# First weights' rounding moved behind two head pairs, the third tile's units on an even grid, and the first pair's differences on VectorE

## The chip, the core and the metric

The kernel runs on one core of one Trainium2 chip. The metric is the device time of one execution in microseconds, lower is better. Before the change it is 1020.40 us in the median of 3 runs (1019.82 to 1021.38).

## The reference

Sliding-window attention over 8 sequences of 576 tokens with 8 heads of 64, followed by a gated feed-forward layer over all 4608 tokens (512 wide, hidden width 1536), all in float32:

```python
scores = scale * np.matmul(q, k.transpose(0, 1, 3, 2))
mask = (rel >= 0) & (rel < window)          # window = 64
scores = np.where(mask, scores, -1000000000.0)
...
out = np.matmul(attn, v)
...
gate = 1.0 / (1.0 + np.exp(-(x @ w_gate)))
val = x @ w_val
return (gate * val @ w_out).astype(np.float32)
```

## The kernel before, in words

The 4608 tokens are cut into 12 tiles of 384. Tiles 0 and 1 are done by plain products; tiles 2 to 11 are done in five pairs, each pair by a Strassen scheme of seven products. Every float32 operand of a large product is split into a rounded part and a remainder, and three matmuls replace one.

**Attention.** A tile has four head pairs; one head pair of one tile is a unit. A unit has three stages. `stage_a` is the scores (`s`, line 201) and the softmax: VectorE masks and finds the minimum (line 219), ScalarE takes the exponentials (line 228), VectorE makes the reciprocals of the sums (lines 234 and 235), and GpSimd multiplies by them (line 237). `stage_b` transposes the result on TensorE (`pp`, line 245), and ScalarE copies it out of PSUM (`pT`, line 250). `stage_c` is the product with V (`oo`, line 262). For tiles 0 and 1 its result is split at once into `x`; for later tiles ScalarE copies it to `xf` (line 269). The PSUM banks of `s`, `pp` and `oo` of tiles 2 and later turn around in one pool of two.

**Weights.** They arrive as 64-bit words and are converted by `conv_a` (ScalarE, lines 111 and 112), `conv_b` (VectorE, lines 120 to 124) and `conv_c` (ScalarE rounds at line 143, VectorE takes the remainder at line 144). The float32 copies are written out again (`w32d`), and for the Strassen scheme `w_sums` reads them back (`a`), makes sums on GpSimd (lines 406 to 409), splits them (lines 143 and 144) and writes them to `wd`, from which `w_load` reads the stationary operands `wt`. All of these DMAs are issued from SyncE's one list.

**Plain tiles.** For tiles 0 and 1 a plan of entries runs over the hidden blocks j: `up` of tile 0 (two halves of 12 matmuls, gate and value, line 297), `down` of tile 0 for the block before (9 matmuls, line 361), `up` of tile 1. The eight units of tiles 2 and 3 are laid between these entries; the numbers say before which entry a stage stands, and .5 means between the two halves. The first unit's transposes stand at 7, which is before the whole `up` of tile 1 for j = 2, its scores at 4.5, its `oo` at 8.

**First Strassen pair.** Tiles 2 and 3 need differences of their `xf` (`x_parts`, lines 424 to 426, and line 434), each of which is then split (`x_split`: line 273 on ScalarE, line 274 on VectorE). The differences `t`, the read-back weights `a`, the converted weights `w32` and the outputs `yo` share one tag of three buffers. The products themselves are line 452, and VectorE adds their parts at line 458.

Each event has a time in the planner (`put`), and the events are written in the order of these times; within an engine a scheduler then settles the list, and `keep_in_program_order` and `issue_after` fix some of it. The change touches `x_parts` and `x_part`, the table of the units' places ahead of `attend`, the time of `conv_c` for the first two weight blocks, and the instruction behind which it must stand.

Of the kernel before, what the change touches and what calls it, by code (L numbers as in the profile page):

```python
# [26 lines left out]
def attn_ffn(ctx: ExitStack, tc: tile.TileContext, qT, kT, vN, w_gate, w_val, w_out, out):  # L27


    nc = tc.nc  # L30
# [48 lines left out]
    marks = {"pT": {}}  # L79
# [191 lines left out]
    def x_split(src, nm, i, eng):  # L271
        x2 = xp.tile([P, 2, TT], F32R, name=f"x_{nm}", tag=f"x{i}")
        hi = nc.scalar.copy(x2[:, 0, :], src)  # L273
        lo = eng.tensor_sub(out=x2[:, 1, :], in0=src, in1=x2[:, 0, :].bitcast(F32))  # L274
        marks[nm] = (hi.ins, lo.ins)
        return x2
# [139 lines left out]
    def t_tile(nm):  # L416
        return mp.tile([P, TT], F32, name=f"t_{nm}", tag="w32", bufs=W32)

    def x_parts(s, c):

        b11, b21, b12, b22 = (xf[(2 * s + b, 2 * a + c)] for b in range(2) for a in range(2))
        t1, t2, t3 = (t_tile(f"{i}_{s}_{c}") for i in range(3))
        eng = nc.gpsimd
        eng.tensor_sub(out=t1, in0=b12, in1=b11)
        eng.tensor_sub(out=t2, in0=b22, in1=t1)
        eng.tensor_sub(out=t3, in0=b22, in1=b12)
        xs[(s, "T", c)] = {"B11": b11, "B21": b21, "B22": b22, "T1": t1, "T2": t2, "T3": t3}

    def x_part(s, n, c):
        src = xs[(s, "T", c)]  # L430
        nm = PRODUCTS[n][1]
        if nm == "T4":
            src["T4"] = src["T2"]
            nc.gpsimd.tensor_sub(out=src["T2"], in0=src["B21"], in1=src["T2"])
        xs[(s, nm, c)] = x_split(src[nm], f"{nm}_{s}_{c}", 2 * n + c, nc.vector)

    def product(s, k, m, n):
# [67 lines left out]
    def put(tm, o, f, *a):  # L505
        events.append((tm, o, f, a))
# [24 lines left out]
    def unit(s, n):  # L531
        return 2 * s + n // 2 % 2, n // 4 + n % 2 * 2

    plan, fill = [], {}
# [5 lines left out]
        if n < NF:  # L540
            plan.append(("up", 1, n))
    at, now = {}, 0.0
    starts = (4, 8, 13, 17, 22, 26, 31, 36, 41)
    for n, (i, nxt) in enumerate(zip(starts, starts[1:])):
        late = 0 if nxt < i + 5 else 0.5 if i + 3 < len(plan) and plan[i + 3][0] == "up" else 1
        for f, x in ((0, i + 0.5), (1, i + 3 + late), (2, nxt)):
            fill.setdefault(x, []).append((f, *unit(1, n)))

    def attend(i):
# [27 lines left out]
    for i in range(KINDS * NF):  # L577
        j, m = divmod(i, KINDS)
        tm = at[("up", 0, max(j, 1))] + ((-10, -2, 6 * j - 0.5) if j < 2 else (-9, -8, 2) if j == 2 else (-14, -12, 2))[m]
        if i < 2:  # L580
            tm = A0 + 11 + 8 * i
        else:
            put(tm - (30 if j == 0 or j == 1 and m < 2 else 6), 2.5, conv_load, i)
        put(tm, 1, conv_a, i)
        put(tm + 2.4, 2, conv_b, i)
        put(tm + 2.5, 2, conv_c, i)

    def last_tile(t, js, ready):

# [17 lines left out]
    for s in range(1, NS):  # L607
        a, b = 2 * s, 2 * s + 1
        for c in range(2):
            put(now - 21 + 10 * c, 5, x_parts, s, c)  # L610
            for n in range(NPR):
                put(now - 19.5 + 10 * c + 1.2 * n, 5.5, x_part, s, n, c)
# [7 lines left out]
        for k in range(NK):  # L620
# [5 lines left out]
            for m in range(2):  # L626
                for n in range(NPR):
                    put(now, 9, product, s, k, m, n)
                    now += PRT
                    if n in (2, 4, 6) and len(downs) > (RESERVE if m else 0) * (k == 1):  # L630
                        j, x = downs.pop(0)
# [11 lines left out]
    for _, _, f, a in events:  # L643
        if f in (conv_a, conv_b, conv_c):
            with ExitStack() as behind:
                j, m = divmod(a[0], KINDS)
                key = j - AHEAD if m < 2 else j - 1
                early = {3: ("1_2",), 2: ("1_3",), 4: ("1_3",), 5: ("1_3",)}.get(a[0], (key,))
                if j == 2 and m < 2:
                    early += tuple(("w", i) for i in (3, 4))  # L650
                for ins in [i for nm in early for i in marks.get(nm, ())]:
                    behind.enter_context(tc.issue_after(ins))
                if a[0] < 2:
                    behind.enter_context(tc.issue_after(marks["pT"][a[0]]))
                f(*a)
        else:
            f(*a)
# [43 lines left out]
```

## Time and profile before

| | us |
|---|---|
| median of 3 runs | 1020.40 |
| the profiled execution, its device time | 1020.06 |
| span of its instructions | 1018.30 |
| TensorE matmuls busy | 985.9 (97%) |
| TensorE weight loads busy | 883.3 (87%) |
| VectorE busy | 662.8 (65%) |
| ScalarE busy | 525.8 (52%) |
| GpSimd busy | 265.7 (26%) |

The span runs from the first instruction to the last; 1.76 us of the device time lie outside it. A busy share is an average over the whole span, so what an engine does in one stage has to be read from a window of that stage. Names in the rows leave the buffer numbers out: `pT` stands for the copies of both heads of all units. "[1.84 <-DVE w L124]" at the end of a row is idle time just before it, and what ended it.

### The profile page before, as it was taken

The numbers are of one execution on the slowest core, as the hardware profiler recorded it, in microseconds if no ns is written. First come the engines' busy times: TensorE is split into PE (matmuls) and PEld (weight loads), VectorE is DVE, ScalarE is ACT, GpSimd is POOL, SyncE is SP. The second block draws the span as 40 slices with busy tenths as digits, with TensorE's granted clock in tenths as the row PEclk, the third lists the DMA queues.
The fourth block names the chain that finished last, engine by engine and source line by source line (L and its number), as shares of the span: only waits on it lengthen the run. The fifth ranks groups of instructions, "written<-read, shape, count | busy, mean of one in ns | idle before, by whom it ended". The sixth has DMA issues, their size and how long they took to land.

```text
span 1018.3 us, 19859 instructions
## 1 busy us (share of the span) xinstructions
PE 985.9 (97%) x6984; PEld 883.3 (87%) x6984; DVE 662.8 (65%) x1810; ACT 525.8 (52%) x1409; POOL 265.7 (26%) x287
## 2 busy tenths in 40 slices
PE   6889999999999999999999999999999999999998
PEld 4689998878899878989988989988989988999996
DVE  6889897637776764756675776675666577344532
ACT  6878886636564544535454654454555454311122
POOL 4200103567662240212132221213212124010100
PEclk9999999999999999999999999999999999999999
DMA  9899886989998624766642776660766652466500
GB/s 303 283 327 363 309 285 214 355 274 355 372 336 295 207 74 153 249 211 216 205 159 74 234 231 204 223 195 32 237 223 215 212 185 73 143 219 204 190 32 32
DMA packets 126243, 221.51 MB, mean 218 GB/s; under 512 B 9408, under 2 KB 82624, under 8 KB 126144
## 3 DMA queue, kind: packets, MB, share of 16 engines
q1 hardware_dynamic: 126144, 220.24, 65.4%
q8 instruction: 56, 0.92, 0.4%
q14 instruction: 43, 0.35, 0.1%
HBM read 178.52 MB, written 41.68 MB: 216 GB/s over the span
## 4 chain that ended last, share of the span: by engine, by line
PE 75%; DVE 7%; DMA 7%; ACT 5%; issue 2%; POOL 2%; SPq 0%; POOLq 0%; DVEq 0%; ACTq 0%
PE pr L452 40%; PE y L361 23%; PE ph L297 4%; PE oo L262 3%; PE s L201 3%; ACT p L228 2%; PE pp L245 2%; DMA wt<-wd 1%; DMA a<-w32d 1%; DVE w L124 1%; DMA w32d<-w 1%; DVE p L219 1%; DMA out_dram<-yo 1%; DVE w L122 1%; DMA hd<-hh 1%
## 5 line engine op out<-in xcount | busy, mean ns | idle before, releaser
L452 PE MATMUL pr<-x_T,wt 128*128 128x384 f32 x1440 | 288.7, 340 | 5.0 <-DVE c L458 3.3
L452 PEld LDWEIGHTS pr<-x_T,wt 128*128 128x128 f32 x1440 | 251.0, 188 | 21.3 <-DVE c L458 5.2
L361 PE MATMUL y<-w,hh 128*128 128x512 f32 x804 | 250.0, 392 | 0.0
L452 PE MATMUL pr<-x_B,wt 128*128 128x384 f32 x1080 | 221.0, 341 | 0.2
L452 PEld LDWEIGHTS pr<-x_B,wt 128*128 128x128 f32 x1080 | 187.9, 188 | 7.8 <-ACT g L307 1.5
L237 POOL TENSOR_TENSOR p<-p,rs 128x384 f32<-128x384 f32 x92 | 79.5, 865 | 401.5 <-DVE rs L235 374.9
L361 PEld LDWEIGHTS y<-w,hh 128*128 128x128 f32 x804 | 148.6, 188 | 21.3 <-ACT hh L326 1.4
L361 PE MATMUL y<-w,hl 128*128 128x512 f32 x402 | 158.6, 395 | 0.7 <-DVE hl L330 0.7
L458 DVE TENSOR_TENSOR u<-pr,p 128x384 f32<-128x384 f32 x120 | 66.6, 555 | 131.9 <-PE pr L452 128.1
L228 ACT ACTIVATE p<-p,mn 128x128 f32<-128x128 f32 x288 | 110.6, 393 | 78.0 <-DVE mn L219 77.8
L330 POOL TENSOR_TENSOR hl<-h,hh 128x384 fp32r<-128x384 f32 x60 | 64.6, 1076 | 240.1 <-DVE hh L328 231.2
L297 PE MATMUL ph<-x,w 128*128 128x384 f32 x576 | 109.6, 343 | 1.7 <-DVE w L144 1.3
L297 PEld LDWEIGHTS ph<-x,w 128*128 128x128 f32 x576 | 100.8, 191 | 4.9 <-DVE w L144 1.6
L361 PEld LDWEIGHTS y<-w,hl 128*128 128x128 f32 x402 | 75.3, 187 | 19.5 <-DVE hl L330 3.4
L219 DVE CUSTOM_DVE_ANT_0 p<-s,m 128x128 f32<-128x128 f32 x288 | 65.3, 285 | 36.1 <-PE s L201 30.6
L463 ACT COPY p<-pr 128x384 f32<-128x384 f32 x60 | 28.3, 471 | 89.6 <-PE pr L452 82.7
L458 DVE TENSOR_TENSOR c<-pr,u 128x384 f32<-128x384 f32 x120 | 66.6, 555 | 12.1 <-PE pr L452 5.8
L250 ACT COPY pT<-pp 128x384 f32<-128x384 f32 x96 | 42.1, 481 | 48.6 <-PE pp L245 48.5
L330 DVE TENSOR_TENSOR hl<-hb,hh 128x384 fp32r<-128x384 f32 x60 | 39.1, 663 | 40.5 <-ACT hh L326 40.0
L311 DVE SCALAR_TENSOR_TENSOR g<-g,e 128x384 f32<-128x384 f32 x96 | 53.7, 571 | 6.8 <-ACT e L308 4.0
L262 PEld LDWEIGHTS oo<-pT,v 128*64 128x64 f32 x1152 | 39.1, 139 | 20.8 <-ACT pT L250 10.7
L274 DVE TENSOR_TENSOR x_T<-t,x_T 128x384 fp32r<-128x384 f32 x40 | 39.3, 999 | 27.1 <-ACT x_T L273 27.1
(73 smaller groups left out, 1212.2 us busy)
## 6 DMA issues: line engine op xcount, KB each, us to landing
wt<-wd SPq DMA_DIRECT2D x210, 512.0 KB, 4.2
v<-in_vN_dram SPq DMA_DIRECT2D x48, 384.0 KB, 4.4
wd<-ws SPq DMA_DIRECT2D x48, 256.0 KB, 4.8
k<-in_kT_dram SPq DMA_DIRECT2D x48, 224.0 KB, 4.2
q<-in_qT_dram SPq DMA_DIRECT2D x48, 192.0 KB, 3.9
wd<-w SPq DMA_DIRECT2D x36, 256.0 KB, 6.5
out_dram<-yo SPq DMA_DIRECT2D x36, 256.0 KB, 2.1
raw<-in_moe_w_gate_dram SPq DMA_DIRECT2D x12, 512.0 KB, 5.4
```

Source lines behind the costliest of these rows:

```text
L219: nc.vector.tensor_tensor_reduce(out=pt[:, u, :], in0=sc[h][:, u, :], in1=masks[key], op0=ALU.add, op1=ALU.min, scale=-SCALE, scalar=3.0e3 ...
L228: exp = nc.scalar.activation(pt[:, u, :], pt[:, u, :], AF.Exp, bias=mn[:, u:u + 1], scale=-1.0, **sums)
L237: eng.tensor_mul(out=pt, in0=pt, in1=rs.unsqueeze(2).broadcast_to([P, UP, P]))
L250: cp = nc.scalar.copy(pT, pp)
L262: pe(nc.tensor.matmul(oo[h * BLK:(h + 1) * BLK, U * BLK:(U + 1) * BLK], vt[:, U, h * BLK:(h + 1) * BLK], pT[h][:, U // 2, half * BLK:(half ...
L274: lo = eng.tensor_sub(out=x2[:, 1, :], in0=src, in1=x2[:, 0, :].bitcast(F32))
L297: pe(nc.tensor.matmul(ph, l, r, start=i == 0, stop=i == len(prs) - 1))
L311: nc.vector.scalar_tensor_tensor(out=g, in0=g, scalar=1.0, in1=e, op0=ALU.add, op1=ALU.mult)
L330: return eng.tensor_sub(out=h_lo, in0=h32, in1=h_hi.bitcast(F32))
L361: pe(nc.tensor.matmul(yb[y], l, r, start=first and n == 0, stop=last and n == 2))
L452: pe(nc.tensor.matmul(ps, l, r, start=new and i == 0, stop=i == len(prs) - 1, skip_group_check=not new))
L458: nc.vector.tensor_add(out=o, in0=ps, in1=a)
```

## The change

Three edits. `conv_c` of the first two weight blocks gets a later time in the planner and must be issued behind the transposes' copy of the head pair after the one named before. The table of places of the eight units is written out; the scores of three units move from between the halves to behind both (8.5 to 9, 17.5 to 18, 26.5 to 27), and the transposes of five units move by half an entry (7 to 7.5, 11.5 to 12, 20.5 to 21, 29.5 to 30, 34.5 to 35). The four differences of `x` for each of the two column halves go to VectorE for the first Strassen pair; the later pairs keep GpSimd.

```diff
@@ -416,11 +416,14 @@
     def t_tile(nm):
         return mp.tile([P, TT], F32, name=f"t_{nm}", tag="w32", bufs=W32)
 
+    def t_engine(s):
+        return nc.vector if s == 1 else nc.gpsimd
+
     def x_parts(s, c):
 
         b11, b21, b12, b22 = (xf[(2 * s + b, 2 * a + c)] for b in range(2) for a in range(2))
         t1, t2, t3 = (t_tile(f"{i}_{s}_{c}") for i in range(3))
-        eng = nc.gpsimd
+        eng = t_engine(s)
         eng.tensor_sub(out=t1, in0=b12, in1=b11)
         eng.tensor_sub(out=t2, in0=b22, in1=t1)
         eng.tensor_sub(out=t3, in0=b22, in1=b12)
@@ -431,7 +434,7 @@
         nm = PRODUCTS[n][1]
         if nm == "T4":
             src["T4"] = src["T2"]
-            nc.gpsimd.tensor_sub(out=src["T2"], in0=src["B21"], in1=src["T2"])
+            t_engine(s).tensor_sub(out=src["T2"], in0=src["B21"], in1=src["T2"])
         xs[(s, nm, c)] = x_split(src[nm], f"{nm}_{s}_{c}", 2 * n + c, nc.vector)
 
     def product(s, k, m, n):
@@ -540,10 +543,9 @@
         if n < NF:
             plan.append(("up", 1, n))
     at, now = {}, 0.0
-    starts = (4, 8, 13, 17, 22, 26, 31, 36, 41)
-    for n, (i, nxt) in enumerate(zip(starts, starts[1:])):
-        late = 0 if nxt < i + 5 else 0.5 if i + 3 < len(plan) and plan[i + 3][0] == "up" else 1
-        for f, x in ((0, i + 0.5), (1, i + 3 + late), (2, nxt)):
+    for n, at_plan in enumerate(((4.5, 7.5, 8), (9, 12, 13), (13.5, 16, 17), (18, 21, 22),
+                                 (22.5, 25, 26), (27, 30, 31), (31.5, 35, 36), (36.5, 40, 41))):
+        for f, x in enumerate(at_plan):
             fill.setdefault(x, []).append((f, *unit(1, n)))
 
     def attend(i):
@@ -583,7 +585,7 @@
             put(tm - (30 if j == 0 or j == 1 and m < 2 else 6), 2.5, conv_load, i)
         put(tm, 1, conv_a, i)
         put(tm + 2.4, 2, conv_b, i)
-        put(tm + 2.5, 2, conv_c, i)
+        put(tm + (2.5 if i > 1 else 3.5), 2, conv_c, i)
 
     def last_tile(t, js, ready):
 
@@ -651,7 +653,7 @@
                 for ins in [i for nm in early for i in marks.get(nm, ())]:
                     behind.enter_context(tc.issue_after(ins))
                 if a[0] < 2:
-                    behind.enter_context(tc.issue_after(marks["pT"][a[0]]))
+                    behind.enter_context(tc.issue_after(marks["pT"][a[0] + (f is conv_c)]))
                 f(*a)
         else:
             f(*a)
```

ScalarE at the first weights, before (`x` and `pT` of unit 0 and 1, the exponentials `p_0_3` of unit 3, `w_0_422` the first rounded weights):

```order
L273 CAST x_0_415<-oo_0_402 128x384
L250 COPY pT_0_1_434<-pp_0_1_430 128x384
L143 CAST w_0_422<-w_0_0_397 128x512
L250 COPY pT_0_1_440<-pp_0_1_436 128x384
L228 ACTIVATE p_0_3_442,rs_0_3_444<-p_0_3_442,mn_0_3_443 128x128 x3
L228 ACTIVATE p_0_3_454<-p_0_3_454,mn_0_3_455 128x128 x3
L111 ACTIVATE w_1_0_548<-raw_0_233 128x512
```

and now:

```order
L273 CAST x_0_415<-oo_0_402 128x384
L250 COPY pT_0_1_428<-pp_0_1_424 128x384
L250 COPY pT_0_1_434<-pp_0_1_430 128x384
L228 ACTIVATE p_0_3_436,rs_0_3_438<-p_0_3_436,mn_0_3_437 128x128 x3
L228 ACTIVATE p_0_3_448<-p_0_3_448,mn_0_3_449 128x128 x3
L143 CAST w_0_475<-w_0_0_397 128x512
L111 ACTIVATE w_1_0_548<-raw_0_233 128x512
```

The rounding `CAST w_0` stood between the two copies `pT_0_1`; it now stands behind both of them and behind the six exponentials of head pair 3.

TensorE at the transposes of the first unit of tile 2, before (`pp_2_0` the transposes, `ph_1_2` the gate and value halves of `up` for tile 1, j = 2):

```order
L245 MATMUL pp_2_0_1183<-ident,p_2_0_1055 128x128 x3
L245 MATMUL pp_2_0_1189<-ident,p_2_0_1067 128x128 x3
L297 MATMUL ph_1_2_1201<-x_0_708,w_2_988 128x384 x3
L297 MATMUL ph_1_2_1201<-x_1_761,w_2_988 128x384 x3
L297 MATMUL ph_1_2_1201<-x_2_835,w_2_988 128x384 x3
L297 MATMUL ph_1_2_1201<-x_3_864,w_2_988 128x384 x3
L297 MATMUL ph_1_2_1218<-x_0_708,w_2_1011 128x384 x3
L297 MATMUL ph_1_2_1218<-x_1_761,w_2_1011 128x384 x3
L297 MATMUL ph_1_2_1218<-x_2_835,w_2_1011 128x384 x3
L297 MATMUL ph_1_2_1218<-x_3_864,w_2_1011 128x384 x3
```

and now:

```order
L297 MATMUL ph_1_2_1183<-x_0_708,w_2_988 128x384 x3
L297 MATMUL ph_1_2_1183<-x_1_761,w_2_988 128x384 x3
L297 MATMUL ph_1_2_1183<-x_2_835,w_2_988 128x384 x3
L297 MATMUL ph_1_2_1183<-x_3_864,w_2_988 128x384 x3
L245 MATMUL pp_2_0_1200<-ident,p_2_0_1055 128x128 x3
L245 MATMUL pp_2_0_1206<-ident,p_2_0_1067 128x128 x3
L297 MATMUL ph_1_2_1218<-x_0_708,w_2_1011 128x384 x3
L297 MATMUL ph_1_2_1218<-x_1_761,w_2_1011 128x384 x3
L297 MATMUL ph_1_2_1218<-x_2_835,w_2_1011 128x384 x3
L297 MATMUL ph_1_2_1218<-x_3_864,w_2_1011 128x384 x3
```

The six transposes moved from ahead of both halves to between them; the product `oo` that follows the second half has not moved.

GpSimd behind the sums of k = 1 of the gate weights (`sw_1`, `ws_0_1`), before (`t_1_0` and `t_1_1` the differences of `x` for the two column halves):

```order
L144 TENSOR_TENSOR ws_0_1_2758<-sw_1_2748,ws_0_1_2758 128x512
L424 TENSOR_TENSOR t_1_0_2876<-xf_0_1758,xf_0_1255 128x384
L425 TENSOR_TENSOR t_1_0_2877<-xf_2_2024,t_1_0_2876 128x384
L426 TENSOR_TENSOR t_1_0_2878<-xf_2_2024,xf_0_1758 128x384
L434 TENSOR_TENSOR t_1_0_2877<-xf_2_1525,t_1_0_2877 128x384
L406 TENSOR_TENSOR sw_1_2896<-a_1_1_2893 128x256
L408 TENSOR_TENSOR sw_1_2896<-a_1_1_2892,a_1_1_2893 128x256
L407 TENSOR_TENSOR sw_1_2896<-sw_1_2896,a_1_1_2892 128x256
L409 TENSOR_TENSOR sw_1_2896<-a_1_1_2892,sw_1_2896 128x256
L144 TENSOR_TENSOR ws_1_1_2901<-sw_1_2896,ws_1_1_2901 128x512
L424 TENSOR_TENSOR t_1_1_3019<-xf_1_2798,xf_1_2257 128x384
L144 TENSOR_TENSOR ws_1_1_2906<-sw_1_2896,ws_1_1_2906 128x512
```

GpSimd now, from the same instruction on:

```order
L144 TENSOR_TENSOR ws_0_1_2746<-sw_1_2736,ws_0_1_2746 128x512
L406 TENSOR_TENSOR sw_1_2896<-a_1_1_2893 128x256
L408 TENSOR_TENSOR sw_1_2896<-a_1_1_2892,a_1_1_2893 128x256
L407 TENSOR_TENSOR sw_1_2896<-sw_1_2896,a_1_1_2892 128x256
L409 TENSOR_TENSOR sw_1_2896<-a_1_1_2892,sw_1_2896 128x256
L144 TENSOR_TENSOR ws_1_1_2901<-sw_1_2896,ws_1_1_2901 128x512
```

VectorE now, for the first column half (`t_1_0` the differences, `x_T_1_0` their remainders):

```order
L427 TENSOR_TENSOR t_1_0_2876<-xf_0_1758,xf_0_1255 128x384
L428 TENSOR_TENSOR t_1_0_2877<-xf_2_2024,t_1_0_2876 128x384
L274 TENSOR_TENSOR x_T_1_0_2939<-t_1_0_2876,x_T_1_0_2939 128x384
L429 TENSOR_TENSOR t_1_0_2878<-xf_2_2024,xf_0_1758 128x384
L274 TENSOR_TENSOR x_T_1_0_2931<-t_1_0_2877,x_T_1_0_2931 128x384
L437 TENSOR_TENSOR t_1_0_2877<-xf_2_1525,t_1_0_2877 128x384
L274 TENSOR_TENSOR x_T_1_0_2950<-t_1_0_2878,x_T_1_0_2950 128x384
L274 TENSOR_TENSOR x_T_1_0_2980<-t_1_0_2877,x_T_1_0_2980 128x384
```

Eight instructions left GpSimd's list, and VectorE's list has each of them ahead of the remainder that needs it.

In the three units whose scores moved, ScalarE's list also has the six conversions of one weight block (lines 111 and 112) ahead of the exponentials that they stood behind.

## Rows read from the trace of the kernel before

**Rows 1.** Busy us (xcount) of PE, PEld, DVE, ACT, POOL; clock; DMA share; GB/s.

```profile
80.00:160.00 80.00, 80.00 (x612) 73.70 (x611) 71.77 (x198) 68.63 (x155) 10.12 (x10) 1.00 0.89 308
```

**Rows 2.** The same view of two stretches at the lower clock.

```profile
20.00:23.30 3.30, 3.30 (x41) 2.85 (x41) 2.47 (x18) 3.30 (x11) 0.83 (x1) 0.50 1.10 346
...
207.70:211.00 3.30, 3.30 (x17) 2.61 (x12) 0.91 (x1) 0.99 (x2) 1.97 (x3) 0.50 0.90 305
```

**Rows 3.** TensorE's waits, 0 to 80 us: total, times, longest.

```profile
PE pp L245 <- POOL p L237: 5.3, 4, 2.8
...
PE oo L262 <- ACT pT L250: 4.3, 4, 2.5
```

**Rows 4.** TensorE's waits, 160 to 300 us: total, times, longest.

```profile
PE oo L262 <- ACT pT L250: 3.3, 3, 1.7
```

**Rows 5.** Timeline of ScalarE, 16 to 22 us (start, length, work, wait).

```profile
16.30 0.46 ACT L250 COPY pT<-pp 128x384 f32<-128x384 f32 x1
18.60 0.62 ACT L143 CAST w<-w 128x512 fp32r<-128x512 f32 x1 [1.84 <-DVE w L124]
...
21.54 0.67 ACT L111 ACTIVATE w<-raw 128x512 f32<-128x512 f32 x1
```

**Rows 6.** Chain that ended last, 19 to 73 us (start, length, step).

```profile
19.60 2.04 ACT p L228 x9
...
31.70 0.88 PE s L201 x22
...
71.28 1.10 POOL p L237
```

**Rows 7.** Timeline of TensorE, 19 to 78 us.

```profile
19.65 1.33 PE L262 MATMUL oo<-pT,v 128*64 128x64 f32 x22 [2.51 <-ACT pT L250]
...
35.75 2.36 PE L297 MATMUL ph<-x,w 128*128 128x384 f32 x12
...
69.12 0.49 PE L245 MATMUL pp<-ident,p 128*128 128x128 f32 x3
72.42 0.55 PE L245 MATMUL pp<-ident,p 128*128 128x128 f32 x3 [2.81 <-POOL p L237]
72.73 4.42 PE L297 MATMUL ph<-x,w 128*128 128x384 f32 x24
77.08 0.92 PE L262 MATMUL oo<-pT,v 128*64 128x64 f32 x24
```

**Rows 8.** Timeline of TensorE, 175 to 240 us.

```profile
175.12 0.88 PE L201 MATMUL s<-k,q 64*64 64x128 f32 x22 [1.45 <-ACT xf L269]
...
193.78 8.46 PE L361 MATMUL y<-w,hb 128*128 128x512 f32 x36
...
206.71 1.46 PE L262 MATMUL oo<-pT,v 128*64 128x64 f32 x24 [1.74 <-ACT pT L250]
208.10 11.90 PE L361 MATMUL y<-w,hb 128*128 128x512 f32 x45
...
223.91 1.23 PE L452 MATMUL pr<-x_B,wt 128*128 128x384 f32 x6
...
239.45 0.91 PE L262 MATMUL oo<-pT,v 128*64 128x64 f32 x22 [0.46 <-ACT pT L250]
```

**Rows 9.** Timeline of GpSimd, first group of differences.

```profile
200.86 1.01 POOL L424 TENSOR_TENSOR t<-xf,xf 128x384 f32<-128x384 f32 x1 [8.58 <-DMA out_dram<-yo]
...
204.74 0.99 POOL L434 TENSOR_TENSOR t<-xf,t 128x384 f32<-128x384 f32 x1 [0.49 <-DVE x_T L274]
```

**Rows 10.** Timeline of ScalarE behind these differences.

```profile
205.76 0.51 ACT L273 CAST x_T<-t 128x384 fp32r<-128x384 f32 x1 [0.97 <-POOL t L434]
206.18 0.85 ACT L250 COPY pT<-pp 128x384 f32<-128x384 f32 x2
```

**Rows 11.** Tile x_T, 195 to 230 us: ns min/median/max.

```profile
L274 DVE TENSOR_TENSOR x_T<-t,x_T x8: 559/1004/1409, 202.4 to 223.9; 128x384 fp32r<-128x384 f32 x8
```

**Rows 12.** ScalarE's groups by line and form, 100 to 160 us.

```profile
L111 ACT ACTIVATE w<-raw 128x512 f32<-128x512 f32 x14 | 9.1, 665 | 0.0
```

## The prediction

> **What bounds the kernel now.** The table of busy times by stretch comes first, because shares of the whole span mix stages. From 80 to 160 us, in the plain tiles, TensorE is busy 80.00 of 80 us, while VectorE has 71.77, ScalarE 68.63 and the DMA engines 0.89 [rows 1]. There TensorE sets the pace and the others have about a tenth to spare. The long Strassen part behind 300 us is not touched by the change, and I carry it over as it is. What can be won are the waits of TensorE in two places, so the lists of its waits come next. Up to 80 us the largest is transposes that wait for GpSimd's product with the reciprocals, 5.3 us in 4 waits, the longest 2.8; then `oo` that waits for ScalarE's copies `pT`, 4.3 us in 4, the longest 2.5 [rows 3]. From 160 to 300 us it is again `oo` for `pT`, 3.3 us in 3 [rows 4]. The timelines then say what stood ahead of the late instruction on its own engine. Each engine takes its list in order here: a row that waits holds back ready work behind it.
>
> **First weights.** ScalarE copies the first half of `pT` at 16.30 us and then stands 1.84 us for the remainder arithmetic of the weights (VectorE, line 124), rounds them in 0.62 us at 18.60, and only then copies the second half [rows 5]. TensorE's `oo` waits 2.51 us for that copy and goes on at 19.65 [rows 7]. In the new list the copy and six exponentials go first, 2.04 us of work [rows 6], which covers the whole 1.84 us. TensorE's own 2.51 us are not what is won: the chain that ended last runs from 19.60 us over these exponentials on ScalarE, through VectorE, to the scores at 31.70 [rows 6]. So ScalarE's idle time is the price, 1.84 us at most and nothing at least, should another link (the loads, or VectorE's list) be late next. The remainder of the weights, which moves back with the rounding, is first needed by the gate products at 35.75 us [rows 7] and is covered. I take **-1.6**, near the upper end, since the following chain consists of compute steps whose inputs come from the same chain.
>
> **Even grid.** The first unit's transposes do three matmuls at 69.12 us and then stand 2.81 us for GpSimd's product, which runs from 71.28; the transposes go on at 72.42 [rows 6, 7]. Behind them 24 matmuls of `up` take 4.42 us before `oo` at 77.08 [rows 7]. Now 12 of them, half of 4.42, 2.2 us, stand ahead of the transposes, and the wait shrinks to 2.81 - 2.2 = 0.6. What is late next is `pT`, which must be copied within the other 2.2 us instead of 4.4; ScalarE is 86% busy there, so a few tenths may come back. Bounds: 0, if the product slips by as much as TensorE gains, and -2.81. I take **-2.0**. The other moved stages stand in the stretch without any wait [rows 1], so there is nothing to gain at once; their risk is the third rival.
>
> Behind 72 us TensorE is then 3.6 us early. It keeps this only if the conversions follow. They are tied to TensorE's progress through the plan, and the tenth to spare on VectorE and ScalarE makes up 3.6 us within 40; I let it pass whole to 160 us.
>
> **Start of the Strassen part.** Scores wait 1.45 us at 175.12 us for `xf`, which stands on ScalarE behind roundings of GpSimd's sums [rows 8]. Three groups of conversions now come ahead of exponentials, the last one just before this place, so the sums can be read back earlier relative to TensorE. Between 0 and -1.45 I take half, **-0.7**.
>
> The differences: GpSimd starts them at 200.86 us when the outputs have left their buffers, and needs until 204.74 + 0.99 = 205.73 us for four [rows 9]. ScalarE rounds the last one at 205.76 and then copies `pT` at 206.18 [rows 10], for which `oo` had stood 1.74 us until 206.71 [rows 8]. On VectorE the last difference is the sixth instruction (four differences, two remainders). The shortest remainder of this size takes 0.559 us [rows 11], six of them 3.35, so it ends at 204.2 instead of 205.7: -1.5. The whole wait of 1.74 is the other end. But the start at 200.86 hangs on outputs that go through SyncE's list behind the writes of the sums, and if these gain less than TensorE, a part of the wait returns; the lower end is 0. I take **-1.1**. For the second half, GpSimd is rid of four more instructions of 1.0 us [rows 9], which only lets sums and weight loads come earlier; at nothing.
>
> The Trainium skill ("SBUF — State Buffer", section "Who interferes with whom") speaks against this move: a VectorE instruction with two inputs in SBUF and a GpSimd instruction that reads SBUF block each other whole. The remainders beside GpSimd's work, 0.559 alone and up to 1.409 us [rows 11], agree with it; by that rule the four differences of the second half, which run beside GpSimd's sums, would give back up to 4 x 0.85 us, and those of the first half nothing, since GpSimd has nothing else to do then.
>
> **Sum.** -1.6 - 2.0 - 0.7 - 1.1 = -5.4. The profiled execution took 1020.06 us (span 1018.30 and 1.76 around it), 0.34 less than the median of 1020.40. 1020.06 - 5.4 = 1014.7, or 1015.0 from the median; I say **1014.8 us**.
>
> **Rivals.**
>
> *The gain is absorbed before the products.* TensorE comes early, but the sums, their write-out and the weight loads form a chain of their own over GpSimd, DMA and SyncE's list. For it speaks that the loads of product weights now stand behind writes of more sums, and that `oo` waits for `pT` behind such roundings again at 239.45 [rows 8]. Against it: the chain starts from conversions that follow TensorE, and GpSimd lost eight instructions. If only half of the first two terms and none of the last two come through, -1.8: 1018.3. Chance 0.20, range 1016.8 to 1019.3, half of it beyond what can be told from no change.
>
> *The low clock goes with the waits.* TensorE was granted 0.50 (1.2 of 2.4 GHz) from 20 to 23.3 and from 207.7 to 211.0 us [rows 2], each just behind one of the waits above. In the second stretch 45 matmuls took 11.90 us, against 36 in 8.46, which is 10.6 for 45 [rows 8]; with `oo` it cost about 1.5. If the wait at 206.71 goes whole (0.6 more than I took) and the low clock with it: -5.4 - 0.6 - 1.5 = -7.5, 1012.6. The Trainium skill ("TensorE: Matmul & The Clock Gate", section "HAM oscillation — how this bites in real kernels") describes this tie of waits to the half rate. Against it: a wait of about a microsecond likely stays there, and the stretch at 20 us is off the chain. Chance 0.17, range 1010.5 to 1012.8.
>
> *Softmax too late in the moved units (slower).* In three units ScalarE now makes six conversions of 0.665 us [rows 12], 4.0 us, ahead of the exponentials, while scores and transposes move by 2.2 us only. The product with the reciprocals comes up to 4.0 us later against transposes 2.2 later. It decides from the point where softmax had less than 1.8 us in hand; if these units end up like the first one, with 2.81 each [rows 7], that is +8.4 - 5.4 = +3.0, 1023.1. Against it: TensorE has no wait at all between 80 and 160 us, and ScalarE has 11 of these 80 us to spare [rows 1]. Chance 0.08.
>
> *The shared access costs what TensorE gains at the products.* By the row of remainders, four differences at 1.409 instead of 0.559 us delay the second half's parts by 3.4 us, about what GpSimd's faster list gives them; then the last two terms are lost: -3.6, 1016.5. The rule that would do this is the one of the Trainium skill's "SBUF — State Buffer" named above. Chance 0.05.
>
> The forecast itself has 0.50, with 1012.8 to 1016.8 as its own range. About 0.2% of the time, 2.0 us, can be told from no change. Faster than 1018.4: 0.50 + 0.17 + 0.05 + half of 0.20 = 0.82. Same: 0.10. Slower: 0.08. The range from 1010.5 to 1019.3 leaves out the slow case and some edges.
>
> **What would show it.** Right: TensorE's `oo` of the second head pair starts near 17.5 us without its 2.5 us wait, the gate products of tile 0 start about 1.6 us earlier than at 35.75 [rows 7]; the wait at the first unit's transposes is below 1 us; TensorE reaches the first Strassen product near 218.5 instead of 223.91 [rows 8]; on VectorE the first four differences last about 0.56 us. Wrong: new waits of `pp` for line 237 or of `oo` for `pT` between 80 and 160 us, or a wait of products for `wt` or `x_T` behind 215 us. If TensorE is early by 3 us at 160 and not at 240, the first rival is it.

## The result, and the profile after

| | before | changed |
|---|---|---|
| median of 20 runs each, us | 1020.02 | 1022.85 |
| lowest to highest, us | 1018.01 to 1025.25 | 1019.74 to 1026.15 |
| profiled execution, us | 1020.06 | 1021.26 |

The ratio is 1.0023 (95% interval 1.0013 to 1.0033): 0.23% slower. The forecast was 1014.8, and its range ended at 1019.3. The waits that the prediction named did shrink, but others came. First TensorE's waits in the changed kernel, from 0 to 80 us and, behind the dots, from 160 to 300 us; they answer to [rows 3, 4].

```profile
PE s L201 <- DMA k<-in_kT_dram: 6.2, 3, 3.9
PE pp L245 <- POOL p L237: 2.7, 3, 1.0
PE oo L262 <- ACT pT L250: 1.0, 2, 0.7
...
PE s L201 <- ACT xf L269: 2.8, 2, 2.6
PE pp L245 <- POOL p L237: 2.6, 2, 1.8
PE oo L262 <- ACT pT L250: 2.2, 1, 2.2
PE pr L455 <- DVE c L461: 1.8, 3, 1.1
```

Up to 80 us `pp` and `oo` wait 3.7 us together instead of 9.6; the scores' wait for the loads of `k` has grown, from 4.9 us to 6.2. Behind 160 us there is a wait of `pp` for GpSimd that [rows 4] did not have, and the scores' wait for `xf` has grown. TensorE's timeline places them and answers to [rows 7, 8] (the last bracket is the wait in front of the row and what ended it):

```profile
16.83 1.82 PE L262 MATMUL oo<-pT,v 128*64 128x64 f32 x24 [0.72 <-ACT pT L250]
34.85 2.35 PE L297 MATMUL ph<-x,w 128*128 128x384 f32 x12
70.27 0.55 PE L245 MATMUL pp<-ident,p 128*128 128x128 f32 x3 [1.02 <-POOL p L237]
131.46 1.29 PE L262 MATMUL oo<-pT,v 128*64 128x64 f32 x24 [1.27 <-ACT pT L250]
174.69 1.55 PE L201 MATMUL s<-k,q 64*64 64x128 f32 x22 [2.58 <-ACT xf L269]
237.18 0.91 PE L262 MATMUL oo<-pT,v 128*64 128x64 f32 x22 [2.20 <-ACT pT L250]
250.13 0.55 PE L245 MATMUL pp<-ident,p 128*128 128x128 f32 x3 [1.83 <-POOL p L237]
268.46 0.55 PE L245 MATMUL pp<-ident,p 128*128 128x128 f32 x3 [0.76 <-POOL p L237]
```

The wait at the first unit's transposes is 1.02 instead of 2.81 us. But at 131 us, in a stretch that had no wait [rows 1], `oo` now waits 1.27 us; the scores wait 2.58 instead of 1.45; and at 250 and 268 us the transposes stand behind GpSimd.

How early TensorE is follows from the same timelines: the start of the n-th matmul of a kind, less that of the same matmul before. `ph` are the gate and value matmuls, `pr` the products; the heads give the start in the kernel before. The experiments are in the same table. Minus is earlier.

| kernel | ratio (95%) | 145th ph 77.92 | 361st ph 134.15 | 541st ph 180.20 | 1st pr 223.91 | 73rd pr 242.38 | 361st pr 318.49 |
|---|---|---|---|---|---|---|---|
| changed | 1.0023 (1.0013-1.0033) | -4.23 | -1.47 | +0.96 | -2.87 | -2.27 | +1.00 |
| e1 weights | 0.9979 (0.9963-0.9994) | -1.20 | -1.20 | -1.47 | -4.41 | -0.98 | -1.34 |
| e2 grid | 0.9999 (0.9984-1.0014) | -3.69 | -0.93 | +1.03 | -2.83 | -1.81 | -1.87 |
| e3 differences | 1.0038 (1.0020-1.0057) | -0.01 | -0.01 | -0.15 | -3.27 | +1.42 | +4.92 |
| e4 weights, grid | 0.9993 (0.9977-1.0008) | -5.52 | -3.01 | +0.74 | -3.11 | -0.53 | -1.33 |
| e5 changed, order mended | 0.9988 (0.9978-0.9997) | -3.16 | -0.76 | -0.36 | -4.22 | -1.14 | -1.43 |
| e6 before, order swapped | 1.0058 (1.0040-1.0076) | +0.48 | +0.48 | -0.16 | -3.22 | -0.31 | +6.06 |
| e7 changed, first half | 0.9973 (0.9962-0.9984) | -4.65 | -2.25 | +0.29 | -3.57 | -1.68 | -2.56 |
| e8 differences, order mended | 1.0000 (0.9989-1.0012) | +0.39 | +0.39 | -0.27 | -3.72 | +0.51 | +0.15 |
| e9 e7, `xf` first | 1.0028 (1.0016-1.0041) | -5.34 | -2.75 | -4.67 | -6.21 | -6.43 | +3.29 |
| e10 e7, `pT` first | 0.9995 (0.9983-1.0007) | -5.36 | -2.80 | -0.23 | -4.08 | -4.59 | -2.64 |
| e11 e7, both first | 1.0028 (1.0013-1.0043) | -4.63 | -2.21 | -4.14 | -5.06 | -5.25 | +2.91 |
| e12 e7, first unit alone | 0.9944 (0.9928-0.9961) | -4.50 | -3.52 | -3.50 | -6.70 | -5.40 | -5.45 |
| e13 weights, first unit | 0.9979 (0.9965-0.9993) | -4.09 | -3.17 | -3.76 | -6.02 | -3.49 | -3.32 |
| e14 later units alone | 1.0045 (1.0029-1.0060) | +1.65 | +4.51 | +8.22 | +4.45 | +9.17 | +8.29 |
| e15 e12, all differences, order mended | 0.9968 (0.9955-0.9981) | -4.62 | -3.72 | +0.10 | -3.75 | -1.74 | -1.98 |

The leads are those of one profiled execution each; the ratios are of the timed runs against runs of the kernel before on the same chip. How much of a lead belongs to the execution and not to an edit is read from e6, whose lists are those of the kernel before on every engine up to 245 us. It is 1.62 us early at the 73rd `ph` (57.65), 0.48 late at the 145th, and 3.22 early at the first product, because `oo` waits 0.35 us there instead of 1.74 [rows 8] and the 45 matmuls behind it take 10.49 us instead of 11.90 (TensorE's timeline of e6):

```profile
205.06 1.29 PE L262 MATMUL oo<-pT,v 128*64 128x64 f32 x24 [0.35 <-ACT pT L250]
206.29 10.49 PE L361 MATMUL y<-w,hb 128*128 128x512 f32 x45
```

So the column of the first product holds about 3 us that the profiled execution of the kernel before lost by itself; the lists of e3 and e8 are unchanged up to 200 us, and they too are 3.27 and 3.72 early. Elsewhere too a lead under 1.6 us in one trace does not by itself show what an edit did. The executions of e2 and e10 are the fastest of their twelve (1018.07 and 1017.79 us), that of e14 is the slowest of its ten (1028.36).

Read the first row from left to right: 4.23 us early at 78 us, 2.8 lost by 134, the rest gone at 180, some of it back at 224, where the kernel before was late, and 3.3 lost between the 73rd and the 361st product. Of the 2.8 us, 1.1 go near 93 us, in the second unit, where no wait is over 0.3 us; what takes them is not shown.

The other losses stand on three lists. At 131 us ScalarE makes six conversions (L111, L112), 3.4 us, directly ahead of both copies `pT`; at 172 us it stands for the load of the last weight ahead of `xf` (ScalarE's timeline of the changed kernel):

```profile
127.58 0.68 ACT L111 ACTIVATE w<-raw 128x512 f32<-128x512 f32 x1
128.16 1.76 ACT L112 ACTIVATE raw<-raw 128x512 int32<-128x512 uint32 x3
129.83 1.21 ACT L111 ACTIVATE w<-raw 128x512 f32<-128x512 f32 x2
130.95 0.83 ACT L250 COPY pT<-pp 128x384 f32<-128x384 f32 x2
...
172.53 0.66 ACT L111 ACTIVATE w<-raw 128x512 f32<-128x512 f32 x1 [1.17 <-DMA raw<-in_moe_w_out_dram]
173.09 0.67 ACT L112 ACTIVATE raw<-raw 128x512 int32<-128x512 uint32 x1
173.66 0.60 ACT L143 CAST ws<-sw 128x512 fp32r<-128x512 f32 x1
174.17 0.47 ACT L269 COPY xf<-oo 128x384 f32<-128x384 f32 x1
```

And at 245 us GpSimd stands 1.97 us for the load of the next weight's sums, with the softmax products (L237) queued behind (GpSimd's timeline of the changed kernel):

```profile
245.43 0.73 POOL L406 TENSOR_TENSOR sw<-a 128x256 f32<-128x256 f32 x1 [1.97 <-DMA a<-w32d]
246.12 0.74 POOL L408 TENSOR_TENSOR sw<-a,a 128x256 f32<-128x256 f32 x1
246.82 0.83 POOL L237 TENSOR_TENSOR p<-p,rs 128x384 f32<-128x384 f32 x1
```

In the kernel before, these products stood ahead of that weight's sums. The clock, which answers to [rows 2] (columns: stretch, its length, busy time and instructions of each engine, granted clock, DMA share, GB/s):

```profile
17.30:27.60 10.30, 8.89 (x108) 7.07 (x109) 9.95 (x45) 9.55 (x33) 4.60 (x5) 0.50 1.12 345
174.40:177.80 3.40, 3.11 (x27) 2.78 (x28) 3.30 (x3) 2.73 (x5) 3.40 (x4) 0.50 1.09 317
```

TensorE had 0.50, its 1.2 GHz level, for 10.3 us at the start, and for 3.4 us around the end of the scores' 2.58 us wait.

### The profile page after: what moved, and what is told of

Its sections match the earlier page's. It is cut to its first block, busy times and chain, and to the rows that moved or that the text cites. A ratio compares the mean times of both kernels' runs of the same rounds, so it can differ in the third digit from the quotient of the medians.

```text
span 1019.5 us, 19854 instructions
## 1 busy us (share of the span) xinstructions
PE 987.0 (97%) x6984; PEld 883.0 (87%) x6984; DVE 665.6 (65%) x1818; ACT 526.4 (52%) x1409; POOL 257.4 (25%) x279
## 4 chain that ended last, share of the span: by engine, by line
PE 82%; DMA 5%; DVE 5%; ACT 3%; issue 2%; SPq 1%; POOL 1%; DVEq 0%; POOLq 0%; ACTq 0%
PE pr L455 40%; PE y L361 26%; PE ph L297 6%; PE oo L262 4%; PE s L201 3%; PE pp L245 2%; DMA wd<-w 1%; DMA raw<-in_moe_w_out_dram 1%; DMA out_dram<-yo 1%; ACT p L228 1%; DMA wd<-ws 1%; DMA k<-in_kT_dram 1%; DVE p L219 1%; DVE w L124 1%; DVE h L493 0%
## 5 line engine op out<-in xcount | busy, mean ns | idle before, releaser
L237 POOL TENSOR_TENSOR p<-p,rs 128x384 f32<-128x384 f32 x92 | 80.1, 872 | 406.8 <-DVE rs L235 299.8
L297 PE MATMUL ph<-x,w 128*128 128x384 f32 x576 | 107.2, 340 | 2.0 <-DVE w L144 1.3
L219 DVE CUSTOM_DVE_ANT_0 p<-s,m 128x128 f32<-128x128 f32 x288 | 65.3, 285 | 34.9 <-PE s L201 29.5
L309 DVE TENSOR_SCALAR g<-g 128x384 int32<-128x384 int32 x96 | 39.1, 412 | 30.3 <-ACT g L307 29.2
L201 PE MATMUL s<-k,q 64*64 64x128 f32 x1152 | 47.6, 296 | 10.2 <-DMA k<-in_kT_dram 6.2
```

The costliest lines, as they stand in the source:

```text
L201: pe(nc.tensor.matmul(sc[h][half * BLK:(half + 1) * BLK, u, :], qt[h * BLK:(h + 1) * BLK, U * BLK:(U + 1) * BLK], kt[h * BLK:(h + 1) * BLK ...
L219: nc.vector.tensor_tensor_reduce(out=pt[:, u, :], in0=sc[h][:, u, :], in1=masks[key], op0=ALU.add, op1=ALU.min, scale=-SCALE, scalar=3.0e3 ...
L237: eng.tensor_mul(out=pt, in0=pt, in1=rs.unsqueeze(2).broadcast_to([P, UP, P]))
L297: pe(nc.tensor.matmul(ph, l, r, start=i == 0, stop=i == len(prs) - 1))
```

## Experiments: the three parts apart

The edits of e1, e2 and e3 are the first, the second and the third part of the diff shown ahead, each alone on the kernel before; e4 has the first two.

**e1.** 

> First part alone (rounding of the first weights behind the second head pair's copy), on the kernel before. Theory 1, the lead is absorbed: TensorE is about 0.9 us early at the first gate product, as in the changed kernel (34.85 against 35.75 us), still early at the first Strassen product, and not at the transposes near 250 us, which follow the write-out of the sums; time 1019 to 1021 us. Theory 2, a part of the change costs by itself: this one is not it, 1018.5 to 1020. If it is (the longer stretch at half clock, 17.3 to 27.6 us), 1022 to 1023.

Measured: 1018.22 us, 0.9979. The part gains about 2 us, a little more than either theory had it. Its lead of 4.4 us at the first product is 1.0 at the 73rd, but e6 goes from 3.2 to 0.3 there without an edit.

**e2.** 

> Even grid alone, on the kernel before. Theory 1: TensorE is 2 to 3 us early from 72 us to about 235 us and within 1 us of the kernel before at 250; 1019 to 1021 us. Theory 2 (the six conversions ahead of the exponentials make softmax late): the waits of oo at 131 us (1.27 in the changed kernel) and of the scores at 174.7 (2.58) are here too, and the time is 1021.5 to 1023.5.

Measured: 1020.45 us, 0.9999. Both theories half hold: the waits at 131 and 174 us are here (the lead goes from -3.69 to +1.03), and yet the time is that of before.

**e3.** 

> Differences of x for the first Strassen pair on VectorE, alone, on the kernel before. Theory 1: the wait of oo at 206.7 us (1.74) is gone, TensorE is 1.7 us or more early at 224 us and within 1 us of the kernel before at 250; 1019 to 1021 us. Theory 3, this part costs (GpSimd's, SyncE's and VectorE's lists between 205 and 300 us are ordered anew, and the new waits at 250 and 268 us come from that): 1021.5 to 1023.5 us, with waits of pp for GpSimd's product near 250 and 268 us.

Measured: 1024.32 us, 1.0038. Theory 3: this part costs. Of the loss, 4.7 us lie between the first and the 73rd product, where e1 and e4 lose 3.4 and 2.6 as well and e6, as yet without an edit, 2.9; and 3.5 us behind it (+1.42 to +4.92), where e1 and e4 lose nothing. There its transposes wait for GpSimd, 0.58 us near 252 us and 0.77 near 270.

**e4.** 

> First weights and even grid together, differences left on GpSimd. Theory 1: early by 3 us at 160 us, within 1 us at 250; 1019 to 1021 us. Theory 2: 1021.5 to 1023.5. Theory 3: 1018 to 1020 us, under the changed kernel by 2 or more.

Measured: 1019.21 us, 0.9993, in the range of theory 1 and of theory 3: without the third part the change is not slower, and not measurably faster either.

## Experiments: GpSimd's order

The four differences of a half and the sums' instructions share GpSimd. Without the differences, the scheduler puts the first two sums of weight 3 ahead of the products of pair 4_2, and those of weight 4 ahead of pair 5_0. GpSimd's list at the first of these places, before on the left, changed on the right:

```
L409 sw_0_3                          L409 sw_0_3
L237 p0_4_2                          L406 sw_1_3
L330 hl_2_6                          L408 sw_1_3
L237 p1_4_2                          L237 p0_4_2
L144 ws0_0_3                         L407 sw_1_3
L144 ws2_0_3                         L330 hl_2_6
L406 sw_1_3                          L237 p1_4_2
L408 sw_1_3                          L409 sw_1_3
```

e5 and e8 queue the sums behind again:

```
+    MULS = {(1, 3): (4, 2), (1, 4): (5, 0)}
...
+        with ExitStack() as behind:
+            if (m, k) in MULS:
+                behind.enter_context(tc.issue_after(marks[("mul",) + MULS[(m, k)]]))
             nc.gpsimd.tensor_add(out=sw[:, 0, :], in0=a2[:, :H], in1=a2[:, H:])
```

(the three `tensor_sub` of the sums stand in the same block). e6 does the opposite to the kernel before: the same products, and the remainders (L144) of the sums made just before, are queued behind these sums. e7 leaves the differences of the second half on GpSimd:

```
-    def t_engine(s):
-        return nc.vector if s == 1 else nc.gpsimd
+    def t_engine(s, c):
+        return nc.vector if s == 1 and c == 0 else nc.gpsimd
```

**e5.** 

> The changed kernel, with GpSimd's sums of two product weights queued behind the softmax products of the head pair that they had passed (weight 3 behind pair 4_2, weight 4 behind pair 5_0), as in the kernel before. Theory 3a (the third part costs because GpSimd, rid of eight differences, is given the next weight's sums ahead of these products, and stands there for the sums' load): the waits of the transposes near 250 us (1.83) and 268 us (0.76) go, the stretch from the 72nd Strassen matmul to the 360th takes 76 to 76.5 us instead of 79.4, and the time falls by 2.5 to 3.5 us, to 1019 to 1020.5. Rival (the loads and writes of the sums set these times, whatever GpSimd's order): the waits move to oo for pT or to products for their sums, and the time stays at 1022 to 1023.

Measured: 1018.76 us, 0.9988. From the 73rd to the 361st product it takes 75.8 us (242.38 - 1.14 to 318.49 - 1.43), the changed kernel 79.4, the kernel before 76.1. GpSimd's timeline of e5 at the same place:

```profile
244.21 0.85 POOL L237 TENSOR_TENSOR p<-p,rs 128x384 f32<-128x384 f32 x1 [0.96 <-ACT p L228]
245.02 1.40 POOL L330 TENSOR_TENSOR hl<-h,hh 128x384 fp32r<-128x384 f32 x1
246.38 0.83 POOL L237 TENSOR_TENSOR p<-p,rs 128x384 f32<-128x384 f32 x1
247.17 0.74 POOL L411 TENSOR_TENSOR sw<-a 128x256 f32<-128x256 f32 x1
```

The product comes at 244.21 instead of 246.82 and waits for the exponentials, not for a load; the transposes wait no more.

**e6.** 

> The kernel before, with all its differences on GpSimd, but with the sums of weights 3 and 4 queued ahead of the same products, as the changed kernel has them: the opposite edit. Theory 3a: a wait of the transposes of 1.5 to 2.5 us near 252 us and one of 0.5 to 1.5 near 270, and 1022.5 to 1024 us. Rival: no change, 1019 to 1020.5.

Measured: 1025.65 us, 1.0058: 0.3 us early at the 73rd product and 6.1 late at the 361st. The waits in TensorE's timeline of e6 stand where they were expected:

```profile
250.66 0.55 PE L245 MATMUL pp<-ident,p 128*128 128x128 f32 x3 [1.19 <-POOL p L237]
252.13 0.55 PE L245 MATMUL pp<-ident,p 128*128 128x128 f32 x3 [0.92 <-POOL p L237]
271.55 0.55 PE L245 MATMUL pp<-ident,p 128*128 128x128 f32 x3 [0.77 <-POOL p L237]
```

So the order alone makes a loss, with every difference still on GpSimd. The mark of the swap is the two waits near 250 us; the third has its like in e2 and e12, whose GpSimd has the order of before there (TensorE's timeline of e12):

```profile
262.61 0.55 PE L245 MATMUL pp<-ident,p 128*128 128x128 f32 x3 [0.76 <-POOL p L237]
```

In e6 the low clock follows as well, 0.54 from 252.4 to 255.8 us and 0.58 from 272.6 to 276.0, where the kernel before and the changed one have 1.00.

**e7.** 

> The changed kernel, but only the first half's four differences on VectorE; those of the second half stay on GpSimd, and its list behind 225 us stands as in the kernel before. Theory 3a: no wait of the transposes for GpSimd near 250 and 268 us, the wait of oo at 206 us stays gone, 1018.5 to 1020 us. Rival (the differences on VectorE cost by themselves): 1021.5 to 1023.

Measured: 1017.61 us, 0.9973, a little under the expectation: faster than both kernels.

**e8.** 

> The third part alone on the kernel before, with the order of the first of these runs. Theory 3a: under the third part alone (1024.3) by 3 us or more, 1019.5 to 1021.5. Rival: 1023.5 to 1025.

Measured: 1020.19 us, 1.0000. The order gives back the 0.38% of e3, and the differences on VectorE alone then win nothing.

## Experiments: where the lead of the first two parts is lost

On e7. e9 queues ScalarE's rounding of the first sums and the last weight's conversion behind the copy `xf` of pair 2_3; e10 queues the rounding of weight 2's sums behind the copies `pT` of pair 4_0; e11 has both. The core of each:

```
+            if (t, p) == (2, 3):                       # e9, in stage_c
+                for i in (0, 2):
+                    queue_behind(marks[("ws", 0, 0, i)], cp)
...
+            if (t, p, h) == (4, 0, 1):                 # e10, in stage_b
+                for i in (0, 2):
+                    queue_behind(marks[("ws", 1, 2, i)], cp.ins)
```

**e9.** 

> On the changed kernel with the differences of the first half alone on VectorE: ScalarE copies xf of head pair 2_3 ahead of the rounding of the first sums and of the last weight's conversion, whose load lands at 171.6 us. Theory A (the lead of the first two parts is lost at 174 us because ScalarE's list holds this copy behind loads): the scores' wait there (2.46 us) and the low clock behind it go, TensorE reaches the 108th down matmul 2 to 4 us earlier than 193.97; at 237 us the wait of oo for pT grows by part of it; time 1015.5 to 1017. Theory B (the sums' loads and writes set the time behind 235 us): early at 194, not at 250: 1017 to 1018.

Measured: 1023.33 us, 1.0028, over both ranges. The step at 174 us is as theory A says: -4.67 instead of +0.29 at the 541st `ph`. Then the lead is lost where theory B says, and more. TensorE's timeline of e9:

```profile
243.17 1.44 PE L464 MATMUL pr<-x_T,wt 128*128 128x384 f32 x6 [3.82 <-DVE c L470]
245.57 2.29 PE L464 MATMUL pr<-x_T,wt 128*128 128x384 f32 x6 [0.95 <-DVE c L470]
```

and ScalarE's, ahead of the exponentials of the next pair, which VectorE's `c` stands behind:

```profile
239.58 0.62 ACT L143 CAST ws<-sw 128x512 fp32r<-128x512 f32 x1 [5.42 <-POOL sw L416]
...
240.91 0.40 ACT L233 ACTIVATE p<-p,mn 128x128 f32<-128x128 f32 x1
```

GpSimd itself had stood 9.4 us for the load `a` there. The edit has also changed SyncE's list: of the two loads that these sums need, the second is issued 0.5 us behind the first in e7, and in e9 6.7 us behind it, after loads of `q`, `k` and `wt`. SyncE's timeline of e7 and, behind the dots, of e9:

```profile
224.65 0.42 SPq L403 DMA_DIRECT2D a<-w32d  x1
225.17 0.73 SPq L404 DMA_DIRECT2D a<-w32d  x1
...
224.80 1.39 SPq L412 DMA_DIRECT2D a<-w32d  x1
231.47 0.33 SPq L413 DMA_DIRECT2D a<-w32d  x1
```

So it is not shown that being early costs this. e12 below is as early at the first product (-6.70, e9 -6.21); its two loads are issued 0.5 us apart, and its GpSimd stands 3.3 us for them.

**e10.** 

> On the same kernel: ScalarE copies both pT of head pair 4_0 ahead of the rounding of weight 2's sums, for whose load GpSimd stands. Theory A2 (the lead at the first product is lost because this copy stands behind the sums): the wait of oo near 236 us goes, the 72nd Strassen matmul comes 1.5 to 3 us earlier than 240.70, 1014.5 to 1016.5 us. Theory B: the wait comes back at 248 to 255 us, where ScalarE's rounding waits for the writes of the sums: 1017 to 1018.

Measured: 1020.02 us, 0.9995. At the 73rd product it is 2.9 us earlier than e7, as A2 has it, and at the 361st 0.1, as theory B has it. In time it is 0.22% slower than e7 and over both ranges; the profiled execution, the fastest of twelve, does not show where.

**e11.** 

> Both edits of the two runs before. Theories A and A2: 1012.5 to 1015 us. Theory B: 1016.5 to 1018, with new waits between 240 and 275 us that take what was won.

Measured: 1022.71 us, 1.0028, over both ranges. As in e9 the second load is issued late, 4.5 us behind the first, and near 244 us products wait 3.9 us for VectorE's `c`.

## Experiments: the grid, unit by unit

e12 is e7, e13 is e1, and e15 is e5, each with the first unit alone on the new grid; e14 is the kernel before with the later units alone (four of them move, three with their scores):

```
+    for n, at_plan in enumerate(((4.5, 7.5, 8), (8.5, 11.5, 13), (13.5, 16, 17), (17.5, 20.5, 22),      # e12, e13, e15
+                                 (22.5, 25, 26), (26.5, 29.5, 31), (31.5, 34.5, 36), (36.5, 40, 41))):
...
+    for n, at_plan in enumerate(((4.5, 7, 8), (9, 12, 13), (13.5, 16, 17), (18, 21, 22),                # e14
+                                 (22.5, 25, 26), (27, 30, 31), (31.5, 35, 36), (36.5, 40, 41))):
```

**e12.** 

> On the same kernel without these two edits, the grid of the third tile changed for its first unit alone (transposes at 7.5 instead of 7), the other units as in the kernel before. The prediction's step (only the first unit's wait counts): within 0.5 us of that kernel, 1017 to 1018.2. Rival (the later units are made late, as the wait of 1.1 us at 131 us says): that wait is gone, TensorE is 1 us or more earlier at 135 us; 1016 to 1017.5.

Measured: 1014.96 us (1013.73 to 1016.80, 6 runs), 0.9944, better than the rival had it and than any other kernel. ScalarE's timeline of e12 in the unit at 131 us of the changed kernel:

```profile
126.02 1.77 ACT L112 ACTIVATE raw<-raw 128x512 int32<-128x512 uint32 x3
127.68 0.47 ACT L250 COPY pT<-pp 128x384 f32<-128x384 f32 x1
128.04 0.63 ACT L143 CAST w<-w 128x512 fp32r<-128x512 f32 x1
128.56 0.49 ACT L250 COPY pT<-pp 128x384 f32<-128x384 f32 x1
128.93 1.26 ACT L111 ACTIVATE w<-raw 128x512 f32<-128x512 f32 x2
```

Two of the six conversions are behind the copies again, the copies have 4.3 us until `oo` instead of 2.3, and `oo` does not wait.

**e13.** 

> First weights and the grid's first unit alone, all differences on GpSimd. Theory D (the first half's differences on VectorE win about 1 us, as the prediction has it): 1 to 2 us over the run with them (0.9944 of before), 1015.5 to 1017. Rival (the wait of oo at 206 us goes with any shift of TensorE, as in the runs without that edit): within 0.5 us of it, 1014.5 to 1015.5.

Measured: 1017.68 us, 0.9979. Theory D in its sign: 0.35% over e12, more than its 1 to 2 us. It is also the ratio of e1: on top of the first weights alone, the first unit's place is not seen in the time.

**e14.** 

> The grid's three later units alone, on the kernel before. Theory (they cost what the first unit wins): waits of oo at 133 us of 1 to 1.5 us, of the scores at 175 us of 2 to 2.6, and 1021.5 to 1023. The prediction's own view (these stages stand in a stretch without waits, nothing gained or lost): 1019.5 to 1020.8.

Measured: 1024.24 us, 1.0045, over the theory's range. TensorE's timeline of e14, in the slowest of its ten runs:

```profile
137.37 1.37 PE L262 MATMUL oo<-pT,v 128*64 128x64 f32 x24 [1.80 <-ACT pT L250]
...
181.78 0.88 PE L201 MATMUL s<-k,q 64*64 64x128 f32 x22 [2.27 <-ACT xf L269]
...
246.37 0.33 PE L262 MATMUL oo<-pT,v 128*64 128x64 f32 x2 [3.70 <-ACT pT L250]
```

and its clock just behind each of them (columns as above):

```profile
138.40:141.80 3.40, 3.40 (x18) 3.29 (x13) 3.40 (x8) 2.03 (x4) 0.00 (x0) 0.50 0.51 153
182.80:186.20 3.40, 3.40 (x12) 3.40 (x12) 3.40 (x12) 2.46 (x5) 3.32 (x4) 0.50 1.03 349
247.60:251.10 3.50, 3.50 (x34) 2.95 (x32) 2.25 (x5) 0.51 (x2) 3.39 (x4) 0.51 0.99 358
```

Here each wait is followed by the low clock: from the 289th `ph` (+2.26) to the 433rd (+5.90) TensorE loses 3.6 us, of which the wait is 1.8.

**e15.** 

> First weights, the grid's first unit alone, all differences on VectorE, and GpSimd's sums behind the softmax products of 4_2 and 5_0. Theory (beside GpSimd's sums the second half's differences take 1.0 to 1.6 us on VectorE instead of 0.56, and cost about 1 us): 1015.5 to 1017. Rival (only GpSimd's order cost): within 0.5 us of the run with the first half alone, 1014.5 to 1015.5.

Measured: 1017.61 us, 0.9968, 0.24% over e12. But its profile loses the lead at 174 us (-3.72 to +0.10, a scores' wait of 2.4 us), ahead of all differences, and takes 75.9 us from the 73rd to the 361st product, where e12 takes 76.1. So the slow differences of the second half are not shown to be the price.

## Why the prediction was wrong

**The failed steps are two that were priced at nothing.** With the parts that the sum did price, and without those two, the time came out as forecast: e12 is 1014.96 us, the forecast was 1014.8. In part that is luck, for the parts have other sizes: the first weights give 0.21% (e1), the first unit on top of them 0.00% (e13), the first half's differences on top of both 0.35% (e12). That is 2.1, 0.0 and 3.6 us, each known to within 1.5 to 2 us, where the sum has 1.6, 2.0 and, with the scores' 0.7, 1.8. From the changed kernel to e7 (second half back on GpSimd) the ratio falls from 1.0023 to 0.9973, 0.50% or 5.1 us; from e7 to e12 (later units back) to 0.9944, 0.29% or 3.0 us.

**"For the second half, GpSimd is rid of four more instructions of 1.0 us [rows 9], which only lets sums and weight loads come earlier; at nothing."** This is the larger one. The sums did come earlier in GpSimd's list: ahead of softmax products on TensorE's path, and there GpSimd stood for the sums' load. e5 (order alone mended, 3.6 us back), e6 (order alone swapped, 0.58% lost) and e8 show it from both sides. None of the rivals named it; the order of the changed list was there to be read beforehand.

**"The other moved stages stand in the stretch without any wait [rows 1], so there is nothing to gain at once; their risk is the third rival."** The third rival, with a chance of 0.08, named these units and their six conversions, and the prediction's own sign of being wrong, a new wait of `oo` for `pT` between 80 and 160 us, came. But the instructions that came late were not the product: they were the copies `pT`, whose time to `oo` the new grid had halved as well (from 4.4 to 2.3 us), and the copy `xf`, which stood behind a load. The wait at 131 us stands in all nine profiles whose later units moved (1.03 to 1.80 us) and in none of the other eight. e14 prices the move at 0.45%, 4.6 us, on the kernel before. "11 of these 80 us to spare" was an average: it said nothing of 3.4 us in a row ahead of a copy due in 2.3.

**First weights, -1.6: right.** The first `ph` comes 1.60 to 1.65 us early in seven of the eleven profiles with this part, and 0.16 to 1.08 in the others; in the six without it, it comes between 0.03 early and 1.89 late. e1 gains 0.21% (0.06 to 0.37).

**First unit, -2.0: right at 78 us, not seen at the end.** The transposes' wait is 1.76 to 3.32 us in the six profiles with the old place and 0 to 1.45 in the eleven with the new one, 2.1 us less in the mean. In time e13 is no faster than e1. The 86% of ScalarE that the term names is its share from 80 to 160 us; behind these transposes, from 72.4 to 77.1, it was busy 2.84 of 4.70 us.

**"I let it pass whole to 160 us": wrong.** In the changed kernel it does not pass the unit at 131 us. In e12 it nearly does (-4.50 to -3.52).

**Scores' wait for `xf`, -0.7: wrong in sign with all units moved.** It grew from 1.45 to 2.58 us. Ahead of the copy stands not only the rounding that the term names but the last weight's conversion, and ScalarE waits 1.17 us for its load. In e12 there is no such wait, and the scores' is 1.45 again. But it is 0.79 in e6, with the lists of before, and 2.35 in e15, whose later units stand as before, so the grid is not shown to be the only cause.

**Differences, -1.1: right in sign, for the first half, but the price came from one execution.** The 1.74 us wait at 206.71 [rows 8] is 0.35 in e6, with the same lists, and with the differences on GpSimd it is 1.15 in e13, 0.47 in e1 and gone in e2, e4 and e14. With the first half on VectorE it is gone in eight of ten profiles and 0.8 in e9 and e11. The first half is worth 0.20% (e4 to e7, where the intervals overlap) and 0.35% (e13 to e12); by what step is open. VectorE's time for one was right: 0.56 us.

**The first rival, gain absorbed before the products (0.20): not shown.** Of the leads at the first product, e1 and e4 keep a quarter or less by the 73rd, e7 half, and e12 5.4 of 6.7 us. But e6 keeps 0.3 of 3.2 us there with no edit ahead of it. Counted from e6, the lead of e1 goes from 1.2 to 0.7 us, and those of e7 and e12 grow, from 0.4 to 1.4 and from 3.5 to 5.1.

**The second, low clock (0.17): both ways.** The stretch at 207.7 us went, as it said, but it is gone in e6 too, with the lists of before (1.00 from 207.7 to 211.0 us); and others came behind the new waits.

**The fourth, shared access (0.05): its row is shown, its price is not.** VectorE's timeline of e3, a difference of each half:

```profile
200.80 0.56 DVE L427 TENSOR_TENSOR t<-xf,xf 128x384 f32<-128x384 f32 x1 [2.62 <-DMA out_dram<-yo]
...
210.91 1.63 DVE L427 TENSOR_TENSOR t<-xf,xf 128x384 f32<-128x384 f32 x1 [2.95 <-POOL sw L409]
```

The first runs with GpSimd idle, the second beside the remainders of GpSimd's sums (L144, from 210.83 us on). The Trainium skill ("SBUF — State Buffer", "Who interferes with whom") has such a pair block each other, and this agrees. The 1.5 us between e5 and e7 may be this; their intervals overlap, and e15 does not bear it out. It stays open.

## What to carry to other kernels

Taking work off an engine also changes what its list does next: look at what moves up, what that waits for, and whose input stands behind it. A stretch without waits is no licence to move stages in it; compare the longest run of work ahead of each moved instruction with the time that it is given. Of several edits in one change, time each alone: here one part alone won 0.2%, another cost 0.4%, and the first with a part of each of the other two won 0.56%. And look at more than one execution before a wait is priced: that of 1.74 us was 0.35 in another one of the same lists.

## What the runs showed of the hardware

Not every wait is followed by the low clock. In e12 TensorE waits 1.45 us at 171.60 and 1.78 us at 233.28, and its clock over 160 to 300 us is full (columns as above):

```profile
160.00:300.00 140.00, 132.99 (x966) 118.21 (x965) 92.10 (x242) 81.61 (x219) 87.31 (x90) 1.00 0.97 333
```

In the changed kernel 2.58 us at 174.69 was followed by it and 2.20 us at 237.18 was not. In e13, whose TensorE, ScalarE and SyncE have the order of e12, a wait of 1.77 us at 233.73 was followed by it (0.55 from 234.8 to 238.2 us). What else decides was not tried.
